# A chunked attention with gated convolution: the first half pair's operands in four loads, one half's row sums on ScalarE, nine zero products, and a new order of the work

## The chip, the cores and the metric

The kernel runs on one NeuronCore of a Trainium2 chip. The metric is the device time of one execution in microseconds (us); lower is better. Engines: TensorE (PE; PEld is its weight load), VectorE (DVE), ScalarE (ACT), GpSimd (POOL), and SyncE (SP), whose queue issues all loads and stores.

## The reference, cut to what matters

```python
scores = q_c @ k_c.T / 8               # chunks of 64 rows, per batch and head; B, H, S, D = 8, 8, 576, 64
scores -= scores.max(-1)
attn = exp(scores); attn /= attn.sum(-1) + 1e-9
x = (attn @ v_c)                       # heads side by side: 4608 rows of 512
gate_pre = sum_k conv_w[k] * x[t - 4 + k]   # five taps, causal within a batch
gate = 1 / (1 + exp(-gate_pre))
out = (gate * (x @ w_val)) @ w_out
```

## The kernel before, in words

The 4608 rows are cut into nine groups g of 512; the 512 columns of x into two pairs p of 256 columns (four heads each), or four blocks m, c of 128. All data is float32. A product that is to be exact is split: x, the gate and both weights are each held as a rounded part (hi) and a remainder (lo), and three products of hi·hi, lo·hi and hi·lo go to TensorE (`V` for x·w_val, `P` for gate·w_out). Group 0 multiplies its first half of x by w_val unsplit instead (`F`).

Nothing in the program loops. `ORDER`, a string of 1127 pieces, is written out by hand; each piece issues one or a few instructions, and each engine runs its own in that order. `SLOTS` is a second table that says which buffer ("home") each tile takes in turn: six `ld` buffers for loads of q, k and v, four `acc` buffers that hold raw weights first and convolution sums later, four PSUM banks `ps`, two PSUM pairs `big`. A load waits on SP until the buffer's last reader is done, and every load behind it waits too.

The pieces that matter here, as `name group pair [half]`:

- `lq`, `lk`, `lv`: loads of queries, keys, values, 512 KB each; `lw n c`: raw weight rows c of w_val (n = v) or w_out (n = o), 512 KB; `lc`: the taps; `st`: a store of 256 KB
- `S` scores (TensorE), `mx` row maximum (VectorE), `sb` subtract it (VectorE), `ex` exp (ScalarE), `sm` row sums and reciprocal (VectorE), `nm` normalise (POOL; `nmD` on VectorE), `T` transpose (TensorE), `ec` copy out (ScalarE), `A` times values (TensorE), `xc`, `xr`, `xd` the copies, the rounded part and the remainder of x. For (0, 0) all of it goes in two halves b
- an alternative to `sb`, `ex`, `sm`: `ng` (VectorE) negates the scaled maximum, `ea` runs exp on ScalarE with the maximum as bias, 64 columns at a time, and lets ScalarE sum each row; `rc` adds 1e-9 and takes the reciprocal. Before, whole pairs (3,0), (4,1), (5,1) and (7,1) go this way
- for (0, 1) the maximum is subtracted on TensorE (`mh`, `ml`, `sp`, then `ep` for the exp), and `xn`, `xe` get the remainder of x there
- `w1` to `w7`, `w6`, `wb n c`: seven elementwise pieces that rebuild one weight chunk from its raw bits and split it. A `G` behind a name puts the piece on POOL, a `D` on VectorE. `F m c` needs the rebuilt chunk c (`w7`), `V m c` its hi (`w6`) and lo (`wb`)
- `k0`, `k` the five taps (`k` on VectorE, 144 of them), `sg` tanh, `vc`, `gs`, `gr`, `gd` the gated product, its rounded part and its remainder, `oc` the copy of a finished output tile
- `W n`: n products of a tile of zeros, whose result nobody reads

Of the kernel before, what the change touches and what calls it, by code (L numbers as in the profile page):

```python
# [21 lines left out]
w4 v 2,lq 1 1,w4 v 1,k0 0 0,w7G v 2,w6 v 2,F 0 3 0,F 0 1 0,sm 0 1,w5 v 1,w7G v 1,A 0 0 1,lv 0 1,S 1 0 0,w1G v 3,
xc 0 0 1,w3G o 3,k 0 0 1,w6 v 0,nmD 0 1,lk 1 1,S 1 0 1,F 0 0 0,T 0 1,mx 1 0,k0 0 1,w5 o 3,F 0 1 1,lw o 0,w5 v 3,
w3 v 3,w1G o 3,F 0 3 1,sb 1 0,ec 0 1,ex 1 0,wb v 2,A 0 1,w2 v 3,k 0 0 4,k 0 0 2,xc 0 1 1,sm 1 0,w1G o 0,xc 0 1 0,
S 1 1 0,w3 o 0,lk 2 0,lq 2 0,xr 0 1,nm 1 0,S 1 1 1,F 0 2 1,k0 0 2,lw o 2,xn 0 1,xe 0 1,mx 1 1,sb 1 1,F 0 0 1,ex 1 1,
w4 v 3,V 0 2 2,V 0 1 2,w7G v 3,k 0 2 3,w5 o 0,sm 1 1,S 2 0 0,S 2 0 1,w3G o 2,w2 o 3,w6 v 3,T 1 0,w6 v 1,ec 1 0,mx 2 0,
V 0 0 2,lk 2 1,V 0 3 2,lq 2 1,lv 1 0,wb v 3,k 0 2 2,lv 1 1,S 2 1 0,sb 2 0,k 0 0 3,S 2 1 1,w2 o 0,ex 2 0,mx 2 1,nm 1 1,
A 1 0,V 0 0 3,k0 0 3,V 0 3 3,xr 1 0,sm 2 0,wb v 0,xc 1 0 1,sb 2 1,vc 0 3,V 0 1 3,V 0 2 3,xc 1 0 0,T 1 1,w1G o 2,
xd 1 0,ex 2 1,V 1 3 0,ec 1 1,sm 2 1,lk 3 0,lq 3 0,vc 0 1,S 3 0 0,S 3 0 1,nm 2 0,k 0 1 2,lw o 1,w2 o 2,wb v 1,A 1 1,
sg 0 0,nm 2 1,xc 1 1 0,V 1 3 1,mx 3 0,lv 2 0,gm 0 0,V 1 1 0,xc 1 1 1,hl 1,lk 3 1,ng 3 0,k 0 2 1,w1G o 1,lk 4 0,  # L30
V 1 1 1,V 1 2 0,xr 1 1,V 1 2 1,xd 1 1,V 1 3 2,w4 o 2,V 1 2 2,V 1 1 2,V 1 3 3,k 0 3 2,V 1 1 3,k 0 2 4,w4 o 0,k 0 1 3,
ea 3 0,k 0 3 4,k 0 1 1,w2 o 1,vc 1 3,T 2 1,lq 3 1,w3G o 1,T 2 0,vc 1 1,rc 3 0,k 0 3 3,w4 o 1,ec 2 0,V 1 0 0,V 1 0 1,
ec 2 1,w5 o 1,S 3 1 0,S 3 1 1,k 0 3 1,A 2 0,V 1 0 2,V 1 2 3,sg 0 2,w5 o 2,k 0 1 4,lq 4 0,mx 3 1,xr 2 0,vc 1 2,w7G o 1,
lv 2 1,sb 3 1,lq 4 1,ex 3 1,V 1 0 3,sg 0 3,k0 1 1,A 2 1,xd 2 0,w4 o 3,V 2 2 0,V 2 3 0,vc 1 0,xc 2 0 0,xc 2 0 1,lq 5 0,
w7 o 0,V 2 3 1,V 2 0 0,gm 0 2,V 2 2 1,V 2 0 1,xr 2 1,lv 3 1,lk 4 1,S 4 0 0,k0 1 2,nm 3 0,sm 3 1,S 4 0 1,gs 0 3,w6 o 1,
xd 2 1,gr 0 2,V 2 2 2,mx 4 0,k0G 1 0,sg 0 1,w7G o 2,k 1 1 3,V 2 0 2,V 2 0 3,w6 o 2,gr 0 0,gs 0 1,gdD 0 0,xc 2 1 0,
xc 2 1 1,sb 4 0,V 2 3 2,w6 o 0,V 2 1 0,w7G o 3,V 2 1 1,w6 o 3,k 1 0 1,S 4 1 0,nm 3 1,S 4 1 1,mx 4 1,k 1 0 4,gr 0 1,
gd 0 2,T 3 1,k 1 1 1,V 2 1 2,k 1 2 2,lv 3 0,vc 2 0,ec 3 1,wb o 0,ng 4 1,wb o 1,k 1 1 4,gdD 0 1,V 2 2 3,lk 5 1,k0 1 3,
k 1 2 3,V 2 1 3,P 0 2 0,vc 2 2,wbD o 2,P 0 1 0,hl 2,k 1 2 1,vc 2 1,k 1 0 3,V 2 3 3,k 1 3 4,k 1 1 2,k 1 3 1,P 0 0 0,
ea 4 1,P 0 0 1,rc 4 1,P 0 2 1,lq 5 1,vc 2 3,P 0 2 2,lk 5 0,P 0 0 2,wbD o 3,k 1 3 3,ex 4 0,T 3 0,k 1 2 4,P 0 1 1,  # L40
ec 3 0,P 0 3 0,A 3 1,k 1 3 2,A 3 0,P 0 3 1,xr 3 1,gr 0 3,k 1 0 2,xr 3 0,xc 3 0 0,sm 4 0,P 0 3 2,xc 3 0 1,P 0 1 2,
gd 0 3,sg 1 3,xcD 3 1 0,P 0 1 3,P 0 0 3,P 0 2 3,xc 3 1 1,sg 1 0,P 0 3 3,xd 3 0,oc 0 1,S 5 0 0,S 5 0 1,oc 0 0,oc 0 2,
xd 3 1,oc 0 3,S 5 1 0,S 5 1 1,V 3 3 0,gs 1 0,V 3 0 0,V 3 2 0,nm 4 1,gr 1 0,k0G 2 2,V 3 0 1,V 3 0 2,V 3 3 1,V 3 2 1,
V 3 0 3,sg 1 2,mx 5 0,V 3 3 2,mx 5 1,V 3 1 0,V 3 1 1,sb 5 0,k0 2 3,nm 4 0,T 4 0,ng 5 1,V 3 2 2,k0 2 1,V 3 2 3,V 3 3 3,
sg 1 1,ea 5 1,T 4 1,vc 3 0,vc 3 3,ec 4 0,gs 1 1,gr 1 1,gd 1 0,P 1 3 0,hl 3,lk 6 0,P 1 2 0,V 3 1 2,k 2 3 2,k 2 2 1,
V 3 1 3,k 2 1 3,lq 6 0,gs 1 2,gr 1 2,k0 3 1,lv 5 0,S 6 0 0,S 6 0 1,ec 4 1,k0G 2 0,k 2 2 2,k 2 0 4,lv 5 1,gs 1 3,
# [10 lines left out]
sg 3 3,k 4 2 2,P 2 1 2,k 4 3 2,P 2 0 3,xc 5 1 0,P 2 2 2,P 2 2 3,oc 2 0,lq 8 1,P 2 1 3,V 5 3 0,P 2 3 2,k 4 3 3,sg 3 0,
k0 5 0,sg 3 2,gs 3 2,k 4 0 2,nm 6 0,P 2 3 3,T 6 0,k 4 1 4,oc 2 1,V 5 0 0,xc 5 1 1,V 5 3 1,V 5 0 1,k0 5 1,gr 3 2,
oc 2 3,gs 3 3,V 4 3 0,sm 6 1,gs 3 0,st 1 2,k0 5 2,ec 6 0,S 7 0 0,S 7 0 1,k 4 1 3,oc 2 2,nmD 6 1,mx 7 0,A 6 0,st 0 1,
V 5 1 0,sb 7 0,V 5 0 2,V 5 1 1,gd 3 2,V 5 1 2,V 5 1 3,gr 3 0,st 1 3,k 4 2 3,gr 3 3,V 4 3 1,V 4 3 2,V 5 0 3,k 4 0 1,  # L60
gd 3 3,vc 5 1,k 4 1 2,V 5 3 2,ex 7 0,gdD 3 1,k 5 1 2,k 4 3 1,vc 5 0,lv 7 0,V 4 3 3,k 4 2 1,lk 8 1,k0 5 3,V 5 3 3,
# [597 lines left out]
```

## Time and profile before

| | us |
|---|---|
| three timed runs, median (lowest to highest) | 266.69 (266.67 to 267.28) |
| the profiled execution | 267.69 |
| its span, first to last instruction | 265.9 |
| TensorE busy in the span | 251.2 |
| VectorE busy | 236.3 |
| ScalarE busy | 188.6 |
| POOL busy | 103.3 |

Starts are microseconds from the span's first instruction. Records of products overlap, since they are pipelined, so the distance between two starts tells TensorE's pace and not the length of one record. Every instruction has the line of one helper (L158), so groups go by the names of tiles: `big` holds scores, transposes and x, `ps` the outputs of `F`, `V`, `P` and `W`, `t` and `t20` to `t2s` are working tiles, `acc` raw weights or convolution sums.

### The profile page before, as it was taken

To read this page: it belongs to the slowest core of one execution; us is meant where nothing else is said; L and a number is where in the kernel's file an instruction comes from. 1 tells how busy PE (TensorE), PEld (TensorE's weight loads), DVE (VectorE), ACT (ScalarE), POOL (GpSimd) and SP (SyncE) were. 2 spreads that over 40 slices of the span, in tenths; PEclk is the share of its full clock that TensorE was granted. 3 is DMA by queue.
4 is the path that set the end of the run, shared out by engine and by line. 5 is a ranking of instruction groups with operands and counts; after the bars stand their busy time and mean duration, and the time that the engine had idled before them with its cause. 6 is when DMAs were issued, how large, how long until landed. Compare 5 with 4: busy or idle time off the path is not lost. (4 is left out here: it accounts for less than half of the span.)

```text
span 265.9 us, 7860 instructions
## 1 busy us (share of the span) xinstructions
PE 251.2 (94%) x3314; PEld 213.7 (80%) x3315; DVE 236.3 (89%) x329; ACT 188.6 (71%) x440; POOL 103.3 (39%) x90
## 2 busy tenths in 40 slices
...
GB/s 226 402 416 395 360 391 273 81 147 179 212 103 147 155 218 20 262 163 78 83 198 31 247 1 188 172 79 2 2 205 192 2 41 4 197 0 0 81 276 158
DMA packets 14291, 42.47 MB, mean 160 GB/s; under 512 B 1712, under 2 KB 1712, under 8 KB 14256
## 3 DMA queue, kind: packets, MB, share of 16 engines
...
q8 instruction: 26, 0.43, 0.7%
...
HBM read 32.53 MB, written 9.44 MB: 158 GB/s over the span
## 5 line engine op out<-in xcount | busy, mean ns | idle before, releaser
L158 DVE SCALAR_TENSOR_TENSOR acc<-x,cw,acc 128x516 f32<-128x516 f32 (+1 forms) x144 | 106.2, 780 | 1.2 <-ACT acc L158 0.8
L158 PE MATMUL ps<-t,v_hi 128*128 128x512 f32 x240 | 82.3, 389 | 0.0
L158 PEld LDWEIGHTS ps<-t,v_hi 128*128 128x128 f32 x240 | 45.2, 189 | 7.1 <-issue 0.2
L158 PE MATMUL ps<-t,v_lo 128*128 128x512 f32 x120 | 45.6, 380 | 0.0
L158 PE MATMUL ps<-o_hi,t 128*128 128x512 f32 x124 | 44.3, 382 | 0.1
L158 PEld LDWEIGHTS big<-ld,ld 64*64 64x64 f32 x1152 | 19.4, 139 | 12.5 <-issue 10.7
L158 PE MATMUL big<-ld,ld 64*64 64x64 f32 x1152 | 21.8, 226 | 7.6 <-DMA ld<-in_q 7.1
L158 POOL TENSOR_TENSOR t<-e_row,rs 128x1024 f32<-128x1024 f32 (+1 forms) x13 | 25.1, 1933 | 8.1 <-DVE rs L158 6.5
L158 DVE TENSOR_REDUCE mx<-big 128x16 f32<-128x1024 f32 (+1 forms) x19 | 21.8, 1153 | 7.1 <-PE big L158 6.9
L158 PEld LDWEIGHTS ps<-o_hi,t 128*128 128x128 f32 x124 | 23.4, 189 | 3.8 <-DVE t2o L158 0.5
L158 ACT COPY x<-big 128x512 f32<-128x512 f32 (+3 forms) x44 | 19.4, 497 | 9.2 <-PE big L158 5.0
L158 PEld LDWEIGHTS ps<-t,v_lo 128*128 128x128 f32 x120 | 22.7, 189 | 3.0 <-issue 0.2
L158 ACT ACTIVATE acc<-x,cw 128x516 f32<-128x516 f32 (+1 forms) x27 | 19.9, 745 | 0.1
L158 ACT ACTIVATE t<-acc 128x512 f32<-128x512 f32 (+7 forms) x35 | 15.6, 505 | 5.9 <-DVE acc L158 2.8
L158 PE MATMUL ps<-o_lo,t 128*128 128x512 f32 x52 | 19.7, 379 | 0.0
L158 ACT ACTIVATE e_row<-big,mx 128x64 f32<-128x64 f32 x64 | 19.1, 363 | 0.6 <-DVE mx L158 0.6
L158 ACT ACTIVATE e_row<-e_row 128x1024 f32<-128x1024 f32 (+1 forms) x14 | 14.0, 1012 | 7.0 <-DVE e_row L158 7.0
L158 PEld LDWEIGHTS big<-t,ld 64*64 64x64 f32 x960 | 15.8, 135 | 3.9 <-issue 1.8
L158 PE MATMUL big<-t,ld 64*64 64x64 f32 x960 | 17.5, 220 | 1.0 <-issue 0.7
L158 ACT ACTIVATE t<-big 128x1024 f32<-128x1024 f32 x13 | 13.4, 1035 | 7.0 <-PE big L158 6.9
L158 DVE TENSOR_REDUCE rs<-e_row 128x16 f32<-128x1040 f32 (+1 forms) x15 | 17.4, 1157 | 0.2
L158 ACT CAST t<-big 128x1024 fp32r<-128x1024 f32 x16 | 16.5, 1033 | 1.2 <-PE big L158 1.2
...
## 6 DMA issues: line engine op xcount, KB each, us to landing
ld<-in_k SPq DMA_DIRECT2D x18, 512.0 KB, 6.0
ld<-in_q SPq DMA_DIRECT2D x18, 512.0 KB, 5.7
ld<-in_v SPq DMA_DIRECT2D x18, 512.0 KB, 5.6
...
acc<-in_moe_w_val SPq DMA_DIRECT2D x4, 512.0 KB, 8.3
acc<-in_moe_w_out SPq DMA_DIRECT2D x4, 512.0 KB, 6.6
...
```

The lines of the kernel that those rows point to most:

```text
L158: return tc.keep_in_program_order(fn(*args, **kwargs))
```

## The change

1. The queries and keys of pair (0, 0) come in four loads of 256 KB, half 1 first, in place of two of 512 KB.
2. Half 1 of pair (0, 0) goes by `ng`, `ea`, `rc` instead of `sb`, `ex`, `sm`; half 0 stays, and is normalised on VectorE.
3. `W 5` between the scores of the first and the second pair becomes `W 6`, and a `W 3` is added between the transposes and the first `A`.
4. `ORDER` and the homes in `SLOTS` are new throughout. Some pieces change engine: over the whole program VectorE gets two more `gd` (19), one `wb`, one `w7`, one half `nm` and one `w3` of w_out, and gives up two `w3` of w_val, two `k0`, one `ec` and one `oc`; POOL gets three more `k0` (9) and two `w3` of w_val, and gives up one `w3` of w_out, two `gd`, one half `nm`, one `w7` and a `wb`. Pair (8, 0) goes by `ea` in place of (7, 1).

The diff, cut; of the two tables the lines that stand first:

```diff
-ORDER = """lk 0 0,lq 0 0,lc,lw v 0,zr 0,w1G c 0,zw,lk 0 1,S 0 0 1,mx 0 0 1,S 0 0 0,zi,sb 0 0 1,mx 0 0 0,ex 0 0 1,zr 1,lq 0 1,
-w5 v 0,sb 0 0 0,lw v 2,W 5,sm 0 0 1,w1G v 0,nm 0 0 1,w3 c 0,zm,ex 0 0 0,w5 c 0,S 0 1 0,w2 v 0,sm 0 0 0,lv 0 0,S 0 1 1,
+ORDER = """lq 0 0 1,lk 0 0 1,lk 0 0 0,zi,lq 0 0 0,zw,S 0 0 1,mx 0 0 1,lc,ng 0 0 1,lw v 0,S 0 0 0,lk 0 1,w3 c 0,W 6,mx 0 0 0,
+w5 c 0,sb 0 0 0,ea 0 0 1,lq 0 1,w3 v 0,lw v 2,w1G c 0,w1G v 0,S 0 1 0,ex 0 0 0,zr 0,zr 1,rc 0 0 1,w5 v 0,nm 0 0 1,
...
-    acc="01230122320301321032013203",
+    acc="01230101212301321023102310",
...
         if (g, p) not in probs:
             probs[g, p] = e_rows[next(e_slot)]
+        if (g, p) not in rss:
             rss[g, p] = tile_of("rs", [P, 16], F32)
...
-    def ea(g, p):
-        for i in range(4):
+    def ea(g, p, b=None):
+        for i in range(4) if b is None else (b, 2 + b):
             ey(g, p, i)
```

What it moves, at three places. First SP's queue from its start; `ld` are the loads' buffers, `acc` the raw weights', and the number behind a buffer's name and before the underscore is its home. Before:

```order
L158 DMA ld0_71<-in_k 128x1024
L158 DMA ld1_73<-in_q 128x1024
L158 DMA raw_cw_75<-in_moe_conv_w 128x40
L158 DMA acc0_77<-in_moe_w_val 128x1024
L158 DMA ld2_83<-in_k 128x1024
L158 DMA ld3_129<-in_q 128x1024
L158 DMA acc1_134<-in_moe_w_val 128x1024
L158 DMA ld4_175<-in_v 128x1024
L158 DMA acc2_195<-in_moe_w_val 128x1024
L158 DMA ld5_201<-in_k 128x1024
L158 DMA ld0_211<-in_q 128x1024
L158 DMA acc3_252<-in_moe_w_out 128x1024
```

After:

```order
L158 DMA ld0_71<-in_q 128x512
L158 DMA ld1_73<-in_k 128x512 x2
L158 DMA ld0_71<-in_q 128x512
L158 DMA raw_cw_101<-in_moe_conv_w 128x40
L158 DMA acc0_104<-in_moe_w_val 128x1024
L158 DMA ld2_123<-in_k 128x1024
L158 DMA ld3_147<-in_q 128x1024
L158 DMA acc1_151<-in_moe_w_val 128x1024
L158 DMA ld4_215<-in_v 128x1024
L158 DMA acc2_225<-in_moe_w_out 128x1024
L158 DMA acc0_293<-in_moe_w_val 128x1024
L158 DMA ld5_298<-in_k 128x1024
```

The first pair's loads are halved, and a w_out chunk (`lw o 0`, into acc2) stands ahead of the third w_val chunk (`lw v 1`), which now takes acc0, the home of the first chunk, so it waits for that chunk's readers. Further down the same queue, two pairs later; before:

```order
L158 DMA ld3_332<-in_k 128x1024
L158 DMA acc2_367<-in_moe_w_out 128x1024
L158 DMA ld4_443<-in_k 128x1024
L158 DMA ld0_445<-in_q 128x1024
L158 DMA acc3_470<-in_moe_w_out 128x1024
L158 DMA ld5_549<-in_k 128x1024
```

After:

```order
L158 DMA acc1_309<-in_moe_w_val 128x1024
L158 DMA ld1_374<-in_v 128x1024
L158 DMA ld2_382<-in_q 128x1024
L158 DMA ld3_384<-in_k 128x1024
L158 DMA ld4_463<-in_q 128x1024
L158 DMA ld0_472<-in_k 128x1024
L158 DMA acc1_482<-in_moe_w_out 128x1024
L158 DMA ld5_505<-in_k 128x1024
```

Here the w_out chunk `acc1_482` (`lw o 3`) takes the home that the w_val chunk `acc1_309` (`lw v 3`) has just had, so it and all behind it wait until `w1`, `w3` and `w5` of that chunk have read it.

Then POOL, from the first normalised half on; `t` are working tiles, `v_lo` the remainder of w_val, `e_row` the exponentials. Before:

```order
L158 TENSOR_TENSOR t40_147<-e_row0_64,rs0_142 128x2x256 x2
L158 TENSOR_SCALAR t24_204<-acc1_134 128x512
L158 MEMSET x0_209 128x4x4
L158 TENSOR_TENSOR ml0_256<-mx1_197,mh0_230 128x16
L158 TENSOR_TENSOR t23_199<-t23_199,t25_206 128x512
L158 TENSOR_TENSOR t27_254<-t27_254,t28_284 128x512
L158 TENSOR_SCALAR t29_323<-acc0_266 128x512
L158 TENSOR_SCALAR t2a_326<-acc3_252 128x512
```

After:

```order
L158 TENSOR_TENSOR t40_181<-e_row0_64,rs0_138 128x2x256
L158 TENSOR_SCALAR t23_199<-acc1_151 128x512
L158 TENSOR_TENSOR ml0_252<-mx1_247,mh0_249 128x16
L158 MEMSET x0_260 128x4x4
L158 TENSOR_SCALAR t28_302<-acc0_293 128x512
L158 TENSOR_SCALAR t29_306<-acc0_293 128x512
L158 TENSOR_TENSOR t29_306<-t29_306,t27_295 128x512
L158 TENSOR_SCALAR t2a_376<-acc1_309 128x512
L158 TENSOR_SCALAR t2c_422<-acc1_309 128x512
L158 TENSOR_TENSOR v_lo_68<-t24_227,v_hi_66 128x512
L158 TENSOR_TENSOR t46_479<-e_row0_64,rs2_460 128x1024
L158 TENSOR_SCALAR t2e_493<-acc2_225 128x512
```

`w7G v 2` (t23_199) has left POOL, and `w1G`, `w3G` and `w7G` of chunk v 1 (t28_302, t29_306 twice) and `w1G`, `w3G` of v 3 (t2a_376, t2c_422) follow each other there, ahead of the remainder of v 2, of `nm 1 0` (t46_479) and of `w3G o 0` (t2e_493).

Last VectorE, around the row sums of pair (0, 1), `rs1`. Before:

```order
L158 TENSOR_SCALAR t27_254<-acc2_195 128x512
L158 SCALAR_TENSOR_TENSOR t23_199<-t24_204,t23_199 128x512
L158 SCALAR_TENSOR_TENSOR t27_254<-t26_228,t27_254 128x512
L158 TENSOR_REDUCE rs1_281<-e_row1_65 128x16
L158 RECIPROCAL rs1_281<-rs1_281 128x16
L158 SCALAR_TENSOR_TENSOR acc1_273<-x0_209,cw_70,acc1_273 128x512
L158 TENSOR_TENSOR t42_330<-e_row1_65,rs1_281 128x1024
L158 TENSOR_REDUCE mx2_361<-big0_306 128x16
```

After:

```order
L158 TENSOR_SCALAR t26_269<-acc2_225 128x512
L158 SCALAR_TENSOR_TENSOR acc3_288<-x0_260,cw_70,acc3_288 128x512
L158 TENSOR_REDUCE rs1_314<-e_row1_65 128x16
L158 RECIPROCAL rs1_314<-rs1_314 128x16
L158 TENSOR_TENSOR t42_318<-e_row1_65,rs1_314 128x1024
L158 SCALAR_TENSOR_TENSOR t29_306<-t28_302,t29_306 128x512
L158 SCALAR_TENSOR_TENSOR acc3_288<-x0_260,cw_70,acc3_288 128x512
L158 TENSOR_REDUCE mx2_369<-big1_325 128x16
```

`w4 v 1` (t27_254 before, t29_306 after) stood ahead of the row sums and the normalising (`nmD 0 1`, t42) of pair (0, 1) and stands behind both.

## Rows read from the trace of the kernel before

**Rows 1.** Stretches (windows): us, busy us and (xcount) per engine, TensorE clock, DMA share, GB/s.

```profile
71.00:241.16 170.16, 170.09 (x2012) 148.70 (x2013) 166.89 (x234) 125.91 (x310) 51.90 (x41) 1.00 0.33 111
...
241.16:262.20 21.04, 20.99 (x96) 18.03 (x96) 8.68 (x12) 6.33 (x12) 3.23 (x2) 1.00 0.37 138
...
262.20:265.90 3.70, 0.00 (x0) 0.00 (x0) 0.00 (x0) 0.59 (x1) 0.00 (x0) 0.85 0.38 142
```

**Rows 2.** TensorE's waits, whole span: tile, releaser, us in total, times, longest.

```profile
PE big L158 <- DMA ld<-in_q: 7.1, 2, 5.5
...
PE big L158 <- issue: 2.1, 3, 0.9
...
PE ps L158 <- POOL t L158: 0.7, 1, 0.7
...
PE big L158 <- POOL x L158: 0.3, 1, 0.3
```

**Rows 3.** Timeline, first 28 us: start, us, engine, operation, count, [idle before].

```profile
5.53 1.99 PE L158 MATMUL big<-ld,ld 64*64 64x64 f32 x64 [5.53 <-DMA ld<-in_q]
...
6.72 0.69 DVE L158 TENSOR_REDUCE mx<-big 128x8 f32<-128x512 f32 x1 [5.61 <-PE big L158]
...
10.88 1.16 PE L158 MATMUL big<-ld,ld 64*64 64x64 f32 x64 [1.54 <-DMA ld<-in_q]
...
12.73 1.09 PE L158 MATMUL ps<-ident,t 128*128 128x128 f32 x8 [0.69 <-POOL t L158]
...
14.08 0.69 PE L158 MATMUL big<-t,ld 64*64 64x64 f32 x32 [0.25 <-ACT t L158]
...
15.67 2.74 PE L158 MATMUL ps<-x,t 128*128 128x512 f32 x6
...
19.04 1.22 DVE L158 TENSOR_TENSOR t<-e_row,rs 128x1024 f32<-128x1024 f32 x1
...
19.41 1.98 POOL L158 TENSOR_TENSOR t<-t,t 128x512 uint32<-128x512 uint32 x1 [1.32 <-ACT t L158]
...
22.32 2.00 POOL L158 TENSOR_SCALAR t2a<-acc 128x512 uint32<-128x512 f32 x1
...
26.98 0.30 PEld L158 LDWEIGHTS big<-t,minus 128*128 128x128 f32 x2 [0.92 <-ACT t L158]
```

**Rows 4.** Loads issued in 0.7:0.9, in 1.2:1.5 and in 4.1:4.4 (us to landing).

```profile
ld<-in_k SPq DMA_DIRECT2D x1, 512.0 KB, 3.4
ld<-in_q SPq DMA_DIRECT2D x1, 512.0 KB, 4.2
ld<-in_v SPq DMA_DIRECT2D x1, 512.0 KB, 9.3
```

**Rows 5.** Page, part 5: ScalarE's activations with a row sum.

```profile
L158 ACT ACTIVATE e_row<-big,mx 128x64 f32<-128x64 f32 x64 | 19.1, 363 | 0.6 <-DVE mx L158 0.6
```

**Rows 6.** TensorE timeline, behind three stops.

```profile
35.94 0.81 PE L158 MATMUL big<-t,ld 64*64 64x64 f32 x39 [0.73 <-issue]
...
43.33 1.16 PE L158 MATMUL big<-t4b,ld 64*64 64x64 f32 x64 [0.92 <-issue]
...
64.89 0.50 PE L158 MATMUL big<-ld,ld 64*64 64x64 f32 x17 [0.50 <-issue]
```

**Rows 7.** Stretches that end at these stops, columns as in rows 1.

```profile
30.70:35.93 5.23, 4.50 (x132) 3.71 (x124) 5.20 (x7) 4.43 (x7) 5.15 (x4) 1.00 1.01 399
35.93:43.32 7.39, 6.47 (x126) 5.29 (x126) 6.69 (x9) 6.46 (x11) 7.07 (x6) 1.00 0.81 304
43.32:64.88 21.56, 21.07 (x382) 18.15 (x381) 19.68 (x28) 19.97 (x58) 14.24 (x11) 1.00 0.50 173
```

**Rows 8.** Page, part 3: the instruction queue (packets, MB, share).

```profile
q8 instruction: 26, 0.43, 0.7%
```

**Rows 9.** VectorE's and TensorE's timelines at the tile t2o.

```profile
75.24 0.68 DVE L158 TENSOR_TENSOR t2o<-t,t2m 128x512 fp32r<-128x512 f32 x1
...
76.76 0.38 PE L158 MATMUL ps<-o_hi,t2o 128*128 128x512 f32 x1
```

More of the change, by code (lines that the diff above doesn't have):

```diff
@@ L22 @@
[L22 to L46, printed above, removed]
@@ L57 @@
[L57 to L61, printed above, removed]
@@ new lines @@
+w5 c 0,sb 0 0 0,ea 0 0 1,lq 0 1,w3 v 0,lw v 2,w1G c 0,w1G v 0,S 0 1 0,ex 0 0 0,zr 0,zr 1,rc 0 0 1,w5 v 0,nm 0 0 1,
+S 0 1 1,w1G v 2,sm 0 0 0,zm,nmD 0 0 0,T 0 0 0,T 0 0 1,lv 0 0,w2 c 0,w2 v 0,W 3,ec 0 0 0,lw o 0,w3 v 2,w2 v 2,A 0 0 0,
+mx 0 1,mh 0 1,w4 v 0,ml 0 1,w4 c 0,w4 v 2,sp 0 1,hl 0,ec 0 0 1,xc 0 0 0,w5 v 2,w9,w7 v 0,w7 v 2,w1 o 0,A 0 0 1,k0 0 0,
+ep 0 1,F 0 2 0,lw v 1,w5 v 1,w6 v 0,lk 1 0,F 0 1 0,w1G v 1,lq 1 0,w3G v 1,k 0 0 3,lw v 3,w2 o 0,F 0 0 0,sm 0 1,w2 v 1,
+nmD 0 1,w4 v 1,w6 v 2,w7G v 1,F 0 3 0,S 1 0 0,k 0 0 2,S 1 0 1,xc 0 0 1,T 0 1,mx 1 0,ec 0 1,sb 1 0,lv 0 1,w1G v 3,
@@ new lines @@
+wbD v 0,w5 v 3,F 0 2 1,lq 1 1,lk 1 1,A 0 1,ex 1 0,xc 0 1 0,F 0 1 1,w3G v 3,S 1 1 0,xr 0 1,k 0 0 1,S 1 1 1,sm 1 0,
+lq 2 0,xc 0 1 1,wb v 2,k0 0 2,k 0 0 4,mx 1 1,lk 2 0,xn 0 1,xe 0 1,F 0 3 1,nm 1 0,w2 v 3,lw o 3,w5 o 0,sb 1 1,V 0 3 2,
+V 0 1 2,w3G o 0,k 0 2 3,T 1 0,lk 2 1,w4 v 3,ex 1 1,w3 o 3,lq 2 1,w7G v 3,sm 1 1,S 2 0 0,nm 1 1,lv 1 0,S 2 0 1,F 0 0 1,
+w5 o 3,V 0 2 2,mx 2 0,ec 1 0,sb 2 0,k0 0 3,S 2 1 0,w6 v 3,lw o 2,w6 v 1,S 2 1 1,wb v 3,sg 0 0,lq 3 0,V 0 0 2,A 1 0,
+w1G o 3,lv 1 1,k0 0 1,w1G o 2,mx 2 1,ex 2 0,sb 2 1,V 0 3 3,xr 1 0,lw o 1,xc 1 0 1,V 0 2 3,T 1 1,sm 2 0,ex 2 1,ec 1 1,
@@ new lines @@
+k 0 3 3,V 0 1 3,V 0 0 3,xd 1 0,lk 3 0,vc 0 3,lq 3 1,A 1 1,w2 o 2,gm 0 0,lk 3 1,xc 1 0 0,V 1 3 0,xr 1 1,w2 o 3,V 1 1 0,
+w5 o 2,S 3 0 0,vc 0 1,sm 2 1,lq 4 1,xd 1 1,wb v 1,S 3 0 1,V 1 3 1,w1G o 1,V 1 1 1,mx 3 0,nm 2 0,V 1 2 0,V 1 3 2,
+w4 o 0,V 1 3 3,xc 1 1 0,V 1 2 1,ng 3 0,xc 1 1 1,k 0 1 3,lv 2 1,V 1 2 2,nm 2 1,k 0 3 2,k 0 2 2,k 0 1 4,lv 2 0,T 2 1,
+gr 0 0,k 0 1 2,V 1 2 3,w4 o 3,k 0 3 4,w3 o 2,ea 3 0,V 1 1 2,V 1 1 3,w3G o 1,lk 4 1,k 0 2 4,T 2 0,k 0 1 1,vc 1 2,hl 1,
+ec 2 1,k 0 3 1,k 0 2 1,V 1 0 0,ec 2 0,w2 o 1,S 3 1 0,S 3 1 1,rc 3 0,vc 1 1,A 2 0,vc 1 3,xr 2 0,sg 0 2,mx 3 1,V 1 0 1,
```

116 lines of the change are left out of this document (66 added, 50 removed).

## The prediction

> **What bounds the kernel now.** First the stretches. From 71 to 241 us TensorE is busy 170.09 of 170.16 us and then 20.99 of 21.04, 0.22 us for each of the last 96 products; behind its last product lie 3.70 us of copy, store and end [rows 1]. So from 71 us on nothing is to be gained but by less work there, and the change takes none away: it adds four products of zeros early and otherwise sorts the same products anew. The time is TensorE's work, plus what it stands still before 71 us, plus that tail. VectorE has 166.89 of the same 170.16 us [rows 1]: it is nearly full too, so a lead that TensorE wins early is kept only if VectorE keeps up.
>
> Next TensorE's waits [rows 2]: 7.1 us for queries (5.5 ahead of the first scores, 1.5 ahead of the second pair's), 0.7 for the first normalised half, 0.3 for POOL, and 2.1 in three stops that the profile puts down to nothing ("issue"). In the timeline these three end at 35.94, 43.33 and 64.89 us, two of them inside a run of equal products that had already begun [rows 6], so no tile can have been missing there. What they share is their distance: up to the first lie 132 + 124 records of products and weight loads from 30.70 us, then 126 + 126, then 382 + 381 [rows 7], that is one, one and three times 256, less a few that are no such records. The instruction queue moved 0.43 MB in 26 packets [rows 8], 16.5 KB each, 64 bytes for each of 256 instructions. I read the stops as TensorE at the end of a block of 256 instructions whose successor had not arrived, with the DMA engines at a share of 1.01 and 0.81 ahead of the first two and 0.50 ahead of the third [rows 7].
>
> The Trainium skill speaks against counting on this: "Runtime: NRT & Kernel Launch", section "Instruction fetch mechanics", has the engine refilled in blocks of 16 KiB, 256 instructions, and calls the cost of crossing a block mostly hidden. The trace agrees with the size of the block and shows a cost of 0.50 to 0.92 us at three crossings. By the Trainium skill's rule term 5 below would be nothing, and the sum +0.7 instead of -1.1.
>
> **The change part by part,** all against the profiled execution (span 265.9, time 267.69; the median of the runs shown is 1.0 lower).
>
> 1. Four half loads. The first keys, issued at 0.7 us, landed 3.4 later, the queries, issued at 1.2, 4.2 later [rows 4]: 512 KB had come by 4.1 us and all by 5.4. Half 1 needs only the first 512 KB, so its scores start near 4.2 in place of 5.53 [rows 3]. Two more issues hold up SP by some 0.8 us, but loads behind queue at the DMA engines anyway (the values, issued in 4.1:4.4, took 9.3 us [rows 4]), so they land when they did: the second pair's scores stay at 10.88, the values at about 13.4. By itself: 0.
>
> 2. Half 1 by `ea`. Maximum at 5.4 (1.19 behind the start of the products, as 6.72 is behind 5.53 [rows 3]), 0.7 for it and 0.2 for `ng`; then eight activations at 19.1/64 = 0.30 us each [rows 5], 2.4 us, to 8.9. Half 0's `ex` queues behind them on ScalarE and ends at 9.5; its sum, reciprocal and `nmD`, 0.7 + 0.2 + 0.7 on VectorE, end near 11.1. Both halves then wait for the second pair's scores (10.88 + 1.16 [rows 3]), so `T` starts at 12.1 in place of 12.73. Behind it `W 3` takes 0.65 us and the values land at 13.4; `A` starts near 13.75 in place of 14.08 [rows 3]: **-0.3**. The cover is that wait for the second pair; without it `ea` would cost its 1.8 us over `ex`. VectorE loses two half operations of 0.69 and gains three small ones.
>
> 3. `A 0 0 1` now stands ahead of the first `F`, and `F` waits for `w7 v 0` behind `mx 0 1`, `w4 v 0` and `w4 v 2` on VectorE. I get `F` at 16.1 with that `A` (0.6) done, against 15.67 [rows 3] with it still to do: parity, so **+0.2**, which leaves -0.1 up to here.
>
> 4. `F 0 2 1`, the first product with chunk v 1. Before, `w7G v 1` began at 19.41 and took 1.98 us [rows 3], just in time. Now `w4 v 1`, on which it waits, stands behind `nmD 0 1`. That began at 19.04 and took 1.22 [rows 3]; the tap that stood ahead of it is gone, so say 18.9 to 20.0, then 0.6 to 0.7 for `w4`, so POOL starts at 20.75. It took 1.98 us in the row; I put the least at two thirds of that, 1.3, an estimate (VectorE was at work on two tiles ahead of and during that row, and may leave POOL more room here): done 22.05 to 22.75. TensorE gets there by 16.1 + four `F` at 0.9 + scores 1.1 + transposes 0.9 = 21.6 at the latest, by a tighter count 21.45, and everything behind `F 0 2 1` on its queue waits. A new stop of 0.6 to 1.4: **+1.0**. The stop of 0.92 in the weight load ahead of `xn` at 26.98 [rows 3] partly goes, since `S 1 1` now stands in front of it: **-0.2**.
>
> 5. The block ends. Counted through the new order (four instructions for a product of scores or values, two for others) they fall again into `A 1 0`, onto the end of `A 1 1` and into `S 4 0`, as the stops do now. What changes is the queue that a block stands in. In the new order `lw o 3` waits for acc1, which `w3G v 3` on POOL reads: behind `w7G v 1`, a short `w1G` and its own 2.00 us (as at 22.32 [rows 3]) that is 25 to 25.5 us, with all loads behind it; `lw o 2` then waits for `w3G o 0`, near 30. So when the blocks for 35 and 42 us are asked for, two to three loads fewer lie ahead, at about 1.3 us each (the values' 9.3 us was a queue of seven). The two first stops should go for the most part, and the third is as likely to stay as to go: of 2.15 us I take **-1.8**; the ends are 0 (no change) and -2.2. The price is what the loads wait for: `lk 3 0` stands behind `lw o 1`, which waits for its buffer until about 36, so it lands near 41, just when `S 3 0` is due. No margin, up to +1 if POOL is late.
>
> 6. Everything later. Over the program VectorE's work falls by some 0.7 us by the list of the change at 0.6 to 0.7 us a half operation, ScalarE's rises by 2 to 3 of which it has plenty, POOL's stays. TensorE stands still nowhere behind 71 us now, so no gain there: 0, with up to +0.7 for a bank that a copy on VectorE frees late. The tail, a copy on ScalarE and a store, is the same: 0.
>
> The sum: -0.1 + 1.0 - 0.2 - 1.8 = **-1.1**, that is 266.6 for such an execution and 265.6 for the median.
>
> **The rivals.** *VectorE takes it back* (same). At 71 us the lead meets the first outputs: the remainder t2o came off VectorE at 75.24 + 0.68 and its product started at 76.76 [rows 9], 0.8 us of slack. In the new order that piece has 1.6 us less VectorE work ahead of it, but TensorE comes 1.9 us of products earlier, plus the lead. So some 0.5 us of lead fits, the rest turns into a stop there unless VectorE's own early idle shrinks alike; time 266.2. For it: 166.89 of 170.16 us; against it: part of VectorE's idle was waiting for TensorE in these stops.
>
> *POOL becomes the bound* (slower). Ahead of `nm 1 0` and the remainder of v 3 it now has two `w3G` of 2.00 us in place of one. If its rows take 1.98 throughout, term 4 is 1.4, the remainder of v 3 comes 0.7 late for `V 0 3 3`, `lk 3 0` lands 1 us late, and only 0.5 of term 5 is left: -0.1 + 1.4 - 0.2 + 0.7 + 1.0 - 0.5 = +2.3; 269.0 for the median; with half of these, 267.9. It decides from the point where `w7G v 1` ends after 23 us. For it: the 1.98 of the row, taken with VectorE at work; against: POOL had a gap of 1.32 ahead of that very row.
>
> *No block is hidden better* (about same, on the upper side): term 5 is nothing, because the stores and loads that do get through fill the DMA engines just as much when a block is asked for: -0.1 + 1.0 - 0.2 = +0.7, 267.4. For it: the third stop came at a DMA share of only 0.50.
>
> *The lead is kept and more:* POOL at 1.3 (+0.6), all stops gone (-2.2), the POOL wait of 0.3 gone: -2.2, 264.5.
>
> **How the numbers follow.** My forecast has 0.40, the larger lead 0.15, VectorE's cap 0.17, no hidden block 0.10, POOL as the bound 0.18. About 0.3%, 0.8 us, is what a measurement of this kernel can tell from no change. A forecast near -1.1 passes that in three of four cases: faster 0.30 + 0.15 + some 0.05 of the cap = 0.50, same 0.30, slower 0.20. The range runs from the larger lead, a little further for its bounds, to POOL with half its price: 263.9 to 267.9.
>
> **What would show it.** Term 1: first scores at 4.2. Term 2: `T` near 12.1, `A` at 13.75. Term 4: a stop of about 1 us ahead of `F 0 2 1`, ended by POOL; none there, or one over 1.5, and it is wrong. Term 5: stops named "issue" of together under 1 us, and a gap of DMA traffic near 25 to 28 us. The cap: TensorE waiting for VectorE between 65 and 80 us. I am wrong altogether if TensorE stands still behind 80 us, where it does not now, or if the tail is longer than 3.7 us.

## The result and the profile after

The changed kernel takes 269.75 us (median of 4 runs, 269.61 to 271.67), the kernel before 266.68 beside it: a ratio of 1.0138, 95% interval 1.009 to 1.0186. It is slower by 3.1 us where 1.1 less was forecast, and above the range. The profiled execution took 271.67 us, 1.9 more than the median. Two executions further down, of 673 us (two loads again, the profiled one) and of 334 us (the taps moved further), lie far outside all others and are left out of every median and reading.

The page's parts on the span and busy time of the changed kernel, then the stretches of [rows 1] in it:

```profile
span 269.9 us, 7886 instructions
...
PE 255.8 (95%) x3319; PEld 215.0 (80%) x3319; DVE 237.9 (88%) x331; ACT 191.2 (71%) x454; POOL 105.6 (39%) x89
```

```profile
71.00:241.16 170.16, 168.90 (x2003) 146.64 (x2003) 167.70 (x233) 126.20 (x308) 60.52 (x44) 1.00 0.32 111
241.16:266.20 25.04, 25.03 (x116) 21.57 (x115) 9.84 (x16) 8.42 (x16) 3.75 (x3) 1.00 0.44 164
266.20:269.90 3.70, 0.00 (x0) 0.00 (x0) 0.00 (x0) 0.59 (x1) 0.00 (x0) 1.00 0.26 100
```

The tail is the same 3.70 us. TensorE is no longer busy without a break between 71 and 241 us: it lacks 1.26 us, where it lacked 0.07. Its waits over the whole span (tile, releaser, us in total, times, longest), to be read beside [rows 2]:

```profile
PE big L158 <- DMA ld<-in_k: 4.4, 1, 4.4
PE big L158 <- DMA ld<-in_q: 2.6, 2, 1.3
PE ps L158 <- POOL t L158: 1.0, 1, 1.0
PE big L158 <- ACT e_row L158: 0.9, 1, 0.9
PE ps L158 <- DVE t2i L158: 0.6, 1, 0.6
PE big L158 <- DVE e_row L158: 0.4, 1, 0.4
PE big L158 <- ACT t2i L158: 0.2, 1, 0.2
```

All three stops named "issue" are gone, the wait of 1.0 for POOL that term 4 foresaw is there, and four waits on VectorE and ScalarE are new. TensorE's timeline, to be read beside [rows 3]:

```profile
4.42 1.13 PE L158 MATMUL big<-ld,ld 64*64 64x64 f32 x32 [4.42 <-DMA ld<-in_k]
6.86 1.13 PE L158 MATMUL big<-ld,ld 64*64 64x64 f32 x32 [1.31 <-DMA ld<-in_q]
7.92 2.74 PE L158 MATMUL ps<-warm 128*128 128x512 bf16 x6
11.92 1.98 PE L158 MATMUL big<-ld,ld 64*64 64x64 f32 x64 [1.25 <-DMA ld<-in_q]
13.84 1.92 PE L158 MATMUL ps<-ident,t 128*128 128x128 f32 x8
...
16.33 0.69 PE L158 MATMUL big<-t,ld 64*64 64x64 f32 x32
...
18.64 3.70 PE L158 MATMUL ps<-x,t 128*128 128x512 f32 x8
...
25.47 1.12 PE L158 MATMUL ps<-x,t 128*128 128x512 f32 x2 [1.01 <-POOL t L158]
```

The first scores start at 4.42 (forecast 4.2). But the second pair's 64 products and the transposes behind them take 1.98 and 1.92 us, where they took 1.16 and 1.09. TensorE goes at half its pace until 15.5 us: the zero products lie 0.43 us apart for 512 columns, which is 1.2 GHz, and later products of 512 columns 0.22, which is 2.4; the column of granted clock says 1.00 all the same. So `A` starts at 16.33 and the first `F` at 18.64.

To compare kernels with different orders I give TensorE's **lost time** at some points: when the first product of a piece starts, less the products of all pieces ahead of it at the pace that they have where nothing waits (1.07 us for a pair's scores, 1.05 for `A`, 0.87 for `T`, 0.86 for `F`, 0.65 for three products of `V` or `P`, 0.92 and 0.56 for `sp` and `xn`; zero products count as nothing, so they are lost time too; the paces are rounded). In two traces of each kernel, and in two of the experiments below:

```
lost us at         before  before   after   after    W 9   W 9 and VectorE's
                           again            again           order mended
S 0 1 (2nd pair)     9.8     9.2    10.9    10.6    10.2      10.3
S 1 0               11.3    11.4    13.9    13.5    11.9      12.4
A 0 1               11.5    11.6    15.3    15.0    12.9      13.6
S 1 1               11.5    11.5    15.6    15.3    14.7      14.9
A 1 0               12.5    12.6    16.4    16.1    15.5      15.7
S 4 1               16.6    14.9    19.0    18.1    17.1      18.0
T 3 0               17.0    15.0    20.5    19.7    18.8      18.1
last product        18.2    16.1    22.2    21.4    20.5      20.2
execution, us      267.69  265.69  271.67  270.87  269.92    269.68
```

The execution less the last line is 249.4 to 249.6 in every column, so the table holds the whole difference. Two parts of it do not hang on the front: behind `S 4 1` (67 to 69 us) the new order loses 3.2 to 3.4 us where the old one loses 1.2 to 1.6; and between `S 1 0` and `S 1 1` it loses 1.7 to 2.8 where the old one loses 0.1 to 0.2.

### The profile page after: what moved, and what is told of

Read it like the earlier page. It is cut to its first block, busy times and chain, and to the rows that moved or that the text cites. A ratio compares the mean times of both kernels' runs of the same rounds, so it can differ in the third digit from the quotient of the medians.

```text
span 269.9 us, 7886 instructions
## 1 busy us (share of the span) xinstructions
PE 255.8 (95%) x3319; PEld 215.0 (80%) x3319; DVE 237.9 (88%) x331; ACT 191.2 (71%) x454; POOL 105.6 (39%) x89
## 4 chain that ended last, share of the span: by engine, by line
PE 79%; ACT 7%; DVE 7%; DMA 3%; issue 1%; SPq 1%; POOL 1%; ACTq 0%; DVEq 0%
PE ps L158 63%; PE big L158 16%; DMA ld<-in_q 3%; ACT e_row L158 2%; DVE mx L158 2%; DVE acc L158 2%; ACT t L158 2%; SPq L158 1%; DVE e_row L158 1%; DVE t L158 1%; POOL t L158 1%; ACT x L158 1%; DVE t2e L158 1%; ACT acc L158 0%; ACT t2j L158 0%
## 5 line engine op out<-in xcount | busy, mean ns | idle before, releaser
L158 PE MATMUL ps<-t,v_hi 128*128 128x512 f32 x216 | 77.4, 393 | 0.0
L158 PEld LDWEIGHTS ps<-t,v_hi 128*128 128x128 f32 x216 | 40.7, 189 | 6.9 <-issue 0.5
L158 PE MATMUL ps<-t,v_lo 128*128 128x512 f32 x104 | 39.5, 380 | 0.0
L158 PE MATMUL ps<-o_hi,t 128*128 128x512 f32 x96 | 35.2, 383 | 0.0
L158 DVE TENSOR_REDUCE mx<-big 128x16 f32<-128x1024 f32 (+1 forms) x19 | 21.8, 1151 | 6.8 <-PE big L158 6.7
L158 ACT COPY t<-ps 128x512 f32<-128x512 f32 x26 | 15.3, 603 | 11.8 <-PE ps L158 8.4
L158 PEld LDWEIGHTS ps<-t,v_lo 128*128 128x128 f32 x104 | 19.7, 189 | 2.7 <-issue 0.5
L158 ACT ACTIVATE t<-big 128x1024 f32<-128x1024 f32 x16 | 16.5, 1044 | 5.7 <-PE big L158 5.7
L158 PEld LDWEIGHTS ps<-o_hi,t 128*128 128x128 f32 x96 | 18.1, 189 | 2.7
L158 POOL TENSOR_SCALAR acc<-x,cw 128x516 f32<-128x516 f32 (+1 forms) x9 | 17.2, 1914 | 4.2 <-ACT x L158 4.2
L158 ACT ACTIVATION_READ_ACCUMULATOR e_row<-big,mx 128x1 f32 x72 | 17.5, 244 | 0.0
```

The source lines that it names most:

```text
L158: return tc.keep_in_program_order(fn(*args, **kwargs))
```

## The experiments

Five theories: A, the half loads as such are slower; B, TensorE's half speed in the front costs the time; C, the chain to `w7G v 1`; D, ends of instruction blocks; E, VectorE's order at 70 to 78 us. The rival to all is that VectorE is full, so that whatever is won is waited away behind it.

**Two loads again (theory A).**

```diff
-lq 0 0 1,lk 0 0 1,lk 0 0 0,zi,lq 0 0 0,zw
+lq 0 0,lk 0 0,zi,zw
```

> The changed kernel with the first queries and keys in two loads of 512 KB again, all else as changed. Theory A (the four half loads move more slowly, and so the second pair's queries land 1.1 us later than before): the second pair's scores start near 10.9 us instead of 11.92, and the time falls by 1.0 or more, to 268.7 at most; if TensorE is then also back at full speed for these scores and the transposes, by 2.6, to 267.1. Rival (VectorE sets the pace behind 50 us, so what is won early is waited away there): scores at 10.9 all the same, but the time stays within 0.5 of 269.75.

269.71 us median of five (269.16 to 272.23), ratio 1.0137 (1.0088 to 1.0187): no gain. It has no usable trace, so where its scores start is not known.

**The kernel before with four loads (theory A).**

```diff
-lk 0 0,lq 0 0,lc
+lk 0 0 1,lq 0 0 1,lk 0 0 0,lq 0 0 0,lc
```

> The kernel before with nothing changed but the first loads: four of 256 KB, half 1 first, in place of two of 512 KB. Theory A (half loads are slower as such): the second pair's scores start near 11.9 in place of 10.88, and the time rises by 1.0, to 267.7; by 2.6, to 269.3, if TensorE falls to half speed there too. Rival (the late landing in the changed kernel comes from its order of issues, not from the size of the loads): scores at 10.9, time 266.7.

266.55 us, ratio 1.000 (0.9966 to 1.0033). The profiled execution has the second pair's scores at 11.64 and at half speed, and took 268.62; the twelve timed ones spread from 265.19 to 268.62, as those of the kernel before do (265.05 to 268.87 in 29). Theory A falls both ways: beside executions that spread over more than 3 us, four loads cost nothing that can be seen, and gain nothing.

**W 9 in place of W 6 (theory B).**

```diff
-W 6,mx 0 0 0
+W 9,mx 0 0 0
```

> The changed kernel with W 9 in place of W 6 between the first and the second pair's scores: three more zero products of 0.43 us fill TensorE's gap from 10.66 to 11.92 us. Theory B (TensorE's speed is halved in the second pair's scores and in the transposes because it stood still ahead of them): the scores take 1.16 instead of 1.98 us, the transposes 1.09 instead of 1.92, the first product of group 0 starts some 1.5 earlier than 18.64, and the time falls to about 268.2. Rival (the speed does not hang on this gap): 1.98 and 1.92 again, 269.75. Second rival (VectorE takes it back later): speed as in B, time within 0.5 of 269.75.

269.50 us (269.29 to 270.02), ratio 1.0116 (1.008 to 1.0153). Scores 1.16, transposes 1.09, first `F` at 16.53, 2.1 earlier than in the first trace of the changed kernel, and the median is 0.25 less. So the half speed can explain why the profiled execution stands 1.9 above its median, not why the median is 3.1 above the kernel before. With the front at full speed (16.53 against the forecast of 16.1) the loss is still there. This trace showed what the changed kernel's had hidden: a stop of 1.36 us inside `A 0 1`.

**w4 v 1 ahead (theory C).**

```diff
-nmD 0 1,w4 v 1,w6 v 2,w7G v 1
+w4 v 1,nmD 0 1,w6 v 2,w7G v 1
```

> The changed kernel with w4 v 1 ahead of nmD 0 1 on VectorE. Theory C (term 4 of the prediction: the first product with weight chunk v 1 waits for POOL, and that for w4 v 1): POOL starts the chunk about 1.1 us earlier than 23.72, the wait of 1.0 ahead of that product falls under 0.3, while the normalised pair (0, 1) comes 0.7 later and its transposes wait 0.4; net -0.5 to -0.8, 269.0 to 269.2. Rival (VectorE takes back later what is won here): the wait is gone, the time within 0.4 of 269.75.

270.89 us, ratio 1.0172 (1.0132 to 1.0211): 1.1 slower than the changed kernel in its own timing. Its timeline:

```profile
22.23 1.07 PE L158 MATMUL big<-ident,t 128*128 128x128 f32 x8 [0.74 <-DVE t L158]
23.26 1.13 PE L158 MATMUL ps<-x,t 128*128 128x512 f32 x2
24.41 1.03 PE L158 MATMUL big<-t,ld 64*64 64x64 f32 x52
25.82 0.45 PE L158 MATMUL big<-t,ld 64*64 64x64 f32 x12 [0.38 <-issue]
```

The wait for POOL is gone, and `T 0 1` in front of it waits 0.74 for the normalised pair instead. POOL was only the messenger: VectorE has `nmD` and `w4` to give at the same time.

**Blocks shifted (theory D).** Behind the `W 6`, 12 products of 2 columns:

```diff
+        for _ in range(small):
+            run(E.matmul, ps[:2, :2], lhsT=warm[:, :2], rhs=warm[:, :2], start=True, stop=True)
```

> The changed kernel with 12 tiny products (2 columns, nobody reads them) behind the W 6, 24 instructions of TensorE more, in its gap ahead of the second pair's scores. Theory D (TensorE stops where a block of 256 instructions ends, if the block behind it has not come): every later end of a block moves 24 instructions forward in the program, so the stop inside A 0 1 (behind 49 of its 64 records in the run with W 9, behind 52 in the run with w4 ahead) moves to 40; and as the block ahead of it now begins in A 0 0 1 in place of an F, there are 3 us more of work in it, so the stop of 0.4 to 1.4 us should be gone: 268.4 to 269.4. Rival (the stop belongs to that product or to what stands in a queue then): it stays behind the same product, 269.75. Second rival (VectorE takes it back at 72 to 78 us): no stop in A 0 1, waits for VectorE there longer, 269.5 or more.

270.41 us, ratio 1.0118 (1.0067 to 1.017). The time says nothing, the timeline much; first this kernel, then W 9 (in the second run of it):

```profile
15.74 0.68 PE L158 MATMUL big<-t,ld 64*64 64x64 f32 x27
17.37 0.34 PE L158 MATMUL big<-t,ld 64*64 64x64 f32 x5 [0.95 <-issue]
...
24.56 0.81 PE L158 MATMUL big<-t,ld 64*64 64x64 f32 x40 [0.25 <-ACT t L158]
25.82 0.58 PE L158 MATMUL big<-t,ld 64*64 64x64 f32 x24 [0.45 <-issue]
```

```profile
23.01 1.12 PE L158 MATMUL ps<-x,t 128*128 128x512 f32 x2 [0.51 <-POOL t L158]
24.07 0.97 PE L158 MATMUL big<-t,ld 64*64 64x64 f32 x49
26.37 0.46 PE L158 MATMUL big<-t,ld 64*64 64x64 f32 x15 [1.34 <-issue]
```

The stop in `A 0 1` comes behind 52 records with `W 6`, behind 49 with three more products (6 instructions: a product and its weight load), behind 40 with twelve more (24 instructions). It sits at a count of instructions, not at a tile: in all eight traces that have this stop, 345 records of products lie ahead of it. And the block end ahead of it, now inside `A 0 0 1`, has a stop of its own, 0.95: the expectation that no stop would be left was wrong.

**The same in the kernel before (theory D)**, 20 small products behind `W 5`:

> The kernel before with 20 tiny products behind the W 5, 40 instructions more, in TensorE's gap ahead of the second pair's scores. Theory D: the stop in A 1 0, behind 25 of its 64 records before, moves to behind 5; the one ahead of A 1 1 moves into S 3 0, about 20 records before its end; the one in S 4 0 goes, since its block now also holds the three V between A 2 0 and A 2 1: 266.2, with the two other stops of 0.5 to 1.3. Rival (stops belong to products): all three where they were, 266.7.

266.08 us, ratio 0.9965 (0.9932 to 0.9998): no slower than the kernel before, and 0.5 us under it at the very edge of the interval. The stop in `A 1 0`:

```profile
35.82 0.33 PE L158 MATMUL big<-t,ld 64*64 64x64 f32 x5
36.65 1.15 PE L158 MATMUL big<-t,ld 64*64 64x64 f32 x59 [0.49 <-issue]
```

It moved from behind 25 records (39 of the 64 were left in [rows 6]) to behind 5, twenty products and forty instructions forward, as expected. The stops ahead of `A 1 1` and in `S 4 0` are gone; for the first a stop in `S 3 0` was expected in its place, and there was none. That they are gone is not the shift's doing alone: the kernel before with four loads, which is not shifted, also stops in `A 1 0` alone, for 1.28 us.

**VectorE's order (theory E).**

```diff
-mx 4 0,gs 0 3,V 2 0 0,V 2 3 3,V 2 2 2,sb 4 0,
+mx 4 0,V 2 0 0,V 2 3 3,V 2 2 2,sb 4 0,gs 0 3,
...
-w6 o 3,k 1 2 4,k 1 0 4,mx 4 1,
+w6 o 3,mx 4 1,
...
-gdD 0 2,P 0 3 1,
+gdD 0 2,k 1 2 4,k 1 0 4,P 0 3 1,
```

> The changed kernel with three VectorE pieces moved: gs 0 3 from ahead of sb 4 0 to behind it, and the taps k 1 2 4 and k 1 0 4 from ahead of gdD 0 1 to behind gdD 0 2. Theory E (the waits of 0.5 for the exponentials' buffer and of 0.6 for t2i between 72 and 78 us come from the order of VectorE's work just there): both waits are gone, and the time falls by 1.0 to 1.3, to 268.6. Rival (VectorE is full as a whole, so what is taken from one wait comes back in another soon behind): waits of about 1 us in other places up to 130 us, time 269.5 or more.

269.38 us, ratio 1.0089 (1.0061 to 1.0116). Both waits are gone, one of 0.35 for `wbD o 3` at 80 us is new, and 2.5 us are lost behind `S 4 1` instead of 3.3.

**Together with the shift and `w7 v 1` on VectorE:**

> Both edits of the two runs above together, and the addition w7 v 1 on VectorE (0.7 us) in place of POOL (1.7 to 2.0 us), so that the first product with chunk v 1 need not wait for POOL. If theories C, D and E hold and nothing is taken back: no wait ahead of that product (-0.6), no stop in A 0 1 (-0.4 to -1.4), no waits at 72 to 78 us (-1.1): 266.6 to 267.6, as the kernel before. Rival (VectorE full): 269 or more, the waits in other places.

269.80 us, ratio 1.012 (1.0083 to 1.0157), from 268.25 to 271.6; the profiled execution is the lowest. It loses 2.5 behind `S 4 1` and has the two stops of the shifted kernel again. Not the 267 of the sum.

**Both kernels once more,** for a second trace of each:

> The kernel before, unchanged, for a second trace. If the difference between the kernels lies where the first traces show it, TensorE loses 1.2 to 1.6 us from the scores of (4,1) to the end here (all that is not product work), as in the three traces with the old order, and it stops where blocks of 256 instructions end: in A 1 0 behind 25 of 64 records, ahead of A 1 1, and in S 4 0, by amounts that may differ.

> The changed kernel, unchanged, for a second trace, hopefully with TensorE at full speed from the second pair's scores on. Expected then: group 0's first product near 16.6 us, a wait of 0.7 to 1.0 for POOL ahead of the first product with chunk v 1, a stop in A 0 1 behind 52 of 64 records, and 3.3 to 3.4 us lost from the scores of (4,1) to the end, as in the three traces with the new order.

265.69 and 270.87 us. The stops in the kernel before, now:

```profile
35.58 0.81 PE L158 MATMUL big<-t,ld 64*64 64x64 f32 x39 [0.27 <-issue]
42.41 1.16 PE L158 MATMUL big<-t4b,ld 64*64 64x64 f32 x64 [0.37 <-issue]
```

The same places, 0.64 us together, no third one and no wait for POOL at 70.89: in [rows 6] they cost 2.15. The profiled execution that the prediction started from was a bad one in just this respect. The second trace of the changed kernel again has half speed in the front; 1.15 for POOL, no stop in `A 0 1` (TensorE comes there 2 us later), one of 0.21 inside `A 1 0`, and 3.3 lost behind `S 4 1`.

**The taps moved further,** behind `wbD o 3`, alone, and then with `W 9` and `w7 v 1` on VectorE:

```diff
-gdD 0 3,P 0 0 0,k 1 3 3,wbD o 3,
+gdD 0 3,P 0 0 0,wbD o 3,k 1 3 3,k 1 2 4,k 1 0 4,
```

> The changed kernel with gs 0 3 behind sb 4 0, and the two taps k 1 2 4 and k 1 0 4 moved further than before, from ahead of gdD 0 1 to behind wbD o 3, so that the remainder of w_out's chunk 3 comes 1.4 us earlier and the wait of 0.35 at 80 us goes too. Theory E: 1.8 to 2.0 us lost from the scores of (4,1) to the end instead of 3.3, and the time at 268.3 to 268.7. Rival (VectorE full): 2.5 or more lost, time at 269.4 or more.

> The same with W 9 in place of W 6 and the addition w7 v 1 on VectorE in place of POOL. If nothing is taken back: no wait ahead of the first product with chunk v 1 (-0.7 to -1.0) and the late waits gone (-1.3): 267.3 to 268.0. Rival (VectorE has no room, and its 0.7 us for w7 v 1 come back as waits by 80 us): 268.5 or more.

269.80 us (ratio 1.0111, 1.0078 to 1.0144) and 269.50 (1.0119, 1.0085 to 1.0154). Both lose 2.3 behind `S 4 1`, but the first median, of five executions from 268.21 to 270.26, is not below the changed kernel's. In the second the wait for POOL is gone, and `xn` at 29.02 waits 0.96 for a copy on ScalarE in its place.

**The edit against its own base.** Since executions spread over 2 us with the front's speed, W 9 with and without the moved pieces on one chip:

> The changed kernel with W 9 alone, once more, as the base for the next run: 269.5 by its first timing, 3.3 to 3.4 us lost from the scores of (4,1) to the end.

> W 9 and the VectorE pieces moved (gs 0 3 behind sb 4 0, the taps k 1 2 4 and k 1 0 4 behind wbD o 3). Theory E: 2.3 us lost from the scores of (4,1) to the end, and 0.8 to 1.1 us less time than the run beside it, about 268.5. Rival (what the edit saves is lost again before the end, or the trace does not tell of the timed executions): within 0.4 of the run beside it.

270.14 us (ratio 1.0122, 1.0088 to 1.0156) and 268.98 (1.0093, 1.0057 to 1.013): the medians differ by 1.16, where the traces have 1.1 less lost behind `S 4 1` (3.4 against 2.3). The timing alone does not settle it: the two intervals overlap, the means of the six and the seven executions differ by only 0.70, and the two traced executions by 0.24. VectorE's timeline without and with the edit:

```profile
67.55 1.22 DVE L158 TENSOR_REDUCE mx<-big 128x16 f32<-128x1024 f32 x1
68.69 1.81 DVE L158 SCALAR_TENSOR_TENSOR t<-t,t2k 128x512 f32<-128x512 f32 x1
70.43 1.21 DVE L158 TENSOR_TENSOR e_row<-big,mx 128x1024 f32<-128x1024 f32 x1
71.56 3.10 DVE L158 SCALAR_TENSOR_TENSOR acc<-x,cw,acc 128x516 f32<-128x516 f32 x3
74.59 1.21 DVE L158 TENSOR_REDUCE mx<-big 128x16 f32<-128x1024 f32 x1
75.72 0.68 DVE L158 TENSOR_TENSOR t2i<-t2a,t2b 128x512 fp32r<-128x512 f32 x1
```

```profile
68.46 1.23 DVE L158 TENSOR_REDUCE mx<-big 128x16 f32<-128x1024 f32 x1
69.79 1.22 DVE L158 TENSOR_TENSOR e_row<-big,mx 128x1024 f32<-128x1024 f32 x1
70.93 0.68 DVE L158 SCALAR_TENSOR_TENSOR t<-t,t2k 128x512 f32<-128x512 f32 x1
71.53 0.75 DVE L158 SCALAR_TENSOR_TENSOR acc<-x,cw,acc 128x516 f32<-128x516 f32 x1
72.19 1.22 DVE L158 TENSOR_REDUCE mx<-big 128x16 f32<-128x1024 f32 x1
73.33 1.73 DVE L158 TENSOR_TENSOR t2i<-t2a,t2b 128x512 fp32r<-128x512 f32 x1
```

And what TensorE waits for in the first of the two:

```profile
71.79 1.07 PE L158 MATMUL big<-ident,t 128*128 128x128 f32 x8 [0.57 <-DVE e_row L158]
...
76.45 0.48 PE L158 MATMUL ps<-o_hi,t2i 128*128 128x512 f32 x1 [0.57 <-DVE t2i L158]
```

`T 3 1` waits for the exponentials' input (`sb 4 0`, which frees its bank), behind a `gs 0 3` of 1.81 us; `P 0 3 1` waits for the remainder t2i (`gdD 0 1`), behind three taps of 3.10. Each starts 0.95 us behind the product ahead of it, where 0.22 is the pace: 0.73 lost, twice. With those pieces behind, neither waits, but a part comes back at 88 us, at the third product of `V 3 1 0`, whose operand comes from VectorE (`xd 3 0`). Without the edit it follows 0.21 us behind its neighbour, with it 0.53:

```profile
87.86 0.38 PE L158 MATMUL ps<-t4b,v_lo 128*128 128x512 f32 x1
88.07 0.38 PE L158 MATMUL ps<-t,v_hi 128*128 128x512 f32 x1
```

```profile
87.16 0.38 PE L158 MATMUL ps<-t4b,v_lo 128*128 128x512 f32 x1
...
87.68 0.19 PEld L158 LDWEIGHTS ps<-t,v_hi 128*128 128x128 f32 x1 [0.55 <-DVE t L158]
87.69 0.48 PE L158 MATMUL ps<-t,v_hi 128*128 128x512 f32 x1
```

So some 1.5 us go and 0.4 come back, 0.3 here and the rest ahead of `T 5 1`. In the traces theory E holds for 1.1 of the 2.0 us, and the rival for the small rest of what was moved. What is left of the 2.0 lies at `T 5 1` (122 us) and `T 7 1` (183 us): by the distances between starts TensorE begins each about 0.3 late, with the edit and without. For the first the mended kernel has a row, a wait of 0.22 for VectorE's `e_row`. These two were not tried by an edit.

The rows of VectorE show one thing more. `gs 0 3` takes 1.81 us without the edit and 0.68 with it, and t2i the other way about, 0.68 and 1.73. The long ones ran while POOL worked on two tiles, without the edit and with it:

```profile
68.67 1.28 POOL L158 TENSOR_TENSOR t2r<-t2r,t2c 128x512 uint32<-128x512 uint32 x1
```

```profile
73.22 1.29 POOL L158 TENSOR_TENSOR o_lo<-t2r,o_hi 128x512 fp32r<-128x512 f32 x1 [2.48 <-ACT o_hi L158]
```

So a piece's place in VectorE's order goes with how long it takes as well; no run moved POOL's pieces alone, so that POOL is the reason is not shown.

## Why the prediction was wrong

**Terms 1 to 3, the front: right in the mechanism.** With TensorE at full speed (second run of W 9) `T` starts at 12.37, `A` at 14.04 and `F` at 16.35, where 12.1, 13.75 and 16.1 were given, each about 0.3 late. (Half 1's own chain, 5.4 + 0.7 + 0.2 + 2.4, ends at 8.7 and not at 8.9; nothing hung on it.) The second pair's scores were to stay at 10.88; in the eleven traces of the new order they start between 10.66 and 11.92, mostly near 11.4. Half speed there, 2 us more in some executions, was not foreseen, and the kernel before has it in some too.

**Term 4: right in size.** 1.0 was given, 1.01 and 1.15 measured, 0.5 to 1.2 in all traces that keep the chain but the shifted kernel's, where TensorE is held up ahead of it and does not wait. (The terms as written add up to 21.7, not 21.6, and the stop to 1.3 at most, not 1.4.) With TensorE at full speed POOL started at 21.26 and took 1.70 us, where 20.75 and 1.3 to 1.98 were given. It named the chain too, but the remedy that it suggests fails: put `w4 v 1` ahead, and `nmD 0 1` is late.

**Term 5: wrong, in three ways.** The stops are ends of instruction blocks, as it read them. But, first, they are worth 2.15 us only in the one execution that was profiled; the three other traces of the old order have 0.64, 1.28 (with four loads) and 0.49 (shifted), so most of the -1.8 was not there to be had in the median. Second, not all of them go: the block end in `A 1 0` stops TensorE in five of the eleven traces of the new order, by 0.16, 0.21, 0.72, 0.81 and 0.87 us, behind 21 of its 64 records with `W 6` and behind 18 with `W 9`. The row of W 9 with VectorE's pieces moved:

```profile
39.14 0.92 PE L158 MATMUL big<-t,ld 64*64 64x64 f32 x46 [0.81 <-issue]
```

The gap in the DMA traffic that was to help is there (a DMA share of 0.50 between 25 and 28 us in this kernel, 0.97 before), but from 34 to 37 us, when that block is fetched, the share is 1.03 again. Third, only the block ends that had stops were followed through the new order; the one in `A 0 1` had none before and got one, 0.4 to 1.4 us in the traces where TensorE is there by 25 us. (An `F` takes four instructions too, not two; eight stand ahead of `A 1 0` in either order, so the count there does not move.)

**Term 6: wrong, and the larger part.** "TensorE stands still nowhere behind 71 us now, so no gain there: 0" took a stretch without waits for one whose order could be changed freely. VectorE was at 166.89 of 170.16 us in it [rows 1], so there was little to absorb an input that moves back in VectorE's order. In place of 0 it cost about 2.0 us: 3.2 to 3.4 are lost behind `S 4 1` in all six traces of the new order without the VectorE edit, 1.2 in three of the four of the old (1.6 in the first), whatever was lost up to there. The term did allow up to 0.7 for a bank that VectorE frees late, which is what `T 3 1` waits for, but left it out of the sum. Nor did VectorE's work fall by 0.7: it was busy for 237.9 and 237.7 us in the two traces of the changed kernel, 236.3 and 236.1 before. The rival "VectorE takes it back" had the place right (65 to 80 us) and the condition wrong: it made the loss depend on a lead.

**The sum,** from the second trace of the kernel before to the second run of W 9, by the table: +0.5 up to `S 1 0`, +0.8 to `A 0 1` (the wait for POOL is 0.5 of it), +1.9 to `S 1 1` (the stop is 1.34 of it), -0.3 to `A 1 0`, -0.7 to `S 4 1` (the stops of before), +2.2 behind it: 4.4, where the two executions differ by 269.92 - 265.69 = 4.23. The medians differ by less, 3.1, as the second trace of the kernel before is one of its better executions; no one trace stands for both medians, so how the 3.1 divide among the terms is not shown to better than these spreads. POOL as the bound, the slower rival, was not it: TensorE waits for POOL no longer than forecast, and no product waits for `lk 3 0`.
